# The first loads of an attention and mixture kernel spread over three queues, with eleven constant products ahead instead of fourteen

## The chip, the cores and the metric

The kernel runs on one core of one Trainium2 chip. The metric is device time in microseconds (us) from one execution; lower is less time. A core has TensorE (PE in the rows, its weight loads PEld), VectorE (DVE), ScalarE (ACT), GpSimd (POOL) and SyncE (SP). SP, ACT and POOL can each issue transfers (DMAs), each into a queue of its own.

## The reference

Three stages follow one another. Attention has batch 4, 12 heads, sequence 448 and head width 64, with capped scores; its output, as 1792 tokens of width 768, goes through a feed-forward layer with a squared ReLU, and that through a soft mixture of 8 experts with 4 slots each.

```python
scores = cap * np.tanh((q @ k.T / 8) / cap)
attn = softmax(scores);  x = attn @ v            # cap is one number, 30.0
g = s * np.maximum(x @ w_in, 0) ** 2 + b;  x = g @ w_out
logits = x @ phi                                  # 32 slots
d = softmax over tokens(logits);  slot_in = d.T @ x
slot_out[e] = np.maximum(slot_in[e] @ w1[e], 0) @ w2[e]
out = softmax over slots(logits) @ slot_out
```

## The kernel before

Two heads make a pair, so there are 24 pairs; for each pair q is a tile of 128 partitions by 448 (224 KB) and k one of 128 by 512 (256 KB). Each is split into a rounded part and a remainder (qh, ql, kh, kl), and a score tile is the sum of three products: kh with qh, kh with ql, kl with qh (`scores`, L148). ScalarE takes the tanh of a score tile (L158) and, when two pairs have delivered theirs, the exponential of both (L220). Sums, weighted values and the feed-forward products follow; the weights of the feed-forward layer are converted on the way (L391 to L430), and the tail reads the expert weights.

What the change touches lies ahead of all that, in `tile_kernel` (from L981). SP issues five loads in this order: `cap` into all 128 partitions (L993), then q and k of pair 0 into `c_tmp` and q and k of pair 1 into `c_hh` (L60, L61 of `load_qk`). DVE fills `c_ones` (L1000), and PE multiplies that constant with itself fourteen times into a PSUM tile that nothing reads (L1004); each product shows as two instructions in the trace. From `cap` DVE works out `c_acap`, the absolute value of cap (L1006, L1007), `c_flag` (whether it is at most 40, L1009), `c_tsc` and `c_eps` (L1011 to L1015, with one exponential on ACT, L1014). POOL issues five small loads: `c_cst`, two parts of `c_misc` (hot and phi), `c_s` and `c_b` (L1017 to L1024).

Every engine then loads `c_flag` into a register (L1035) and branches on it: one of two bodies runs, and nothing of a body runs ahead of that branch. In the body, `prep_pair` (L119 to L134) splits pairs 0 and 1 in parts: on DVE the order is qh and the first quarter of kh of pair 0, ql, the first quarter of kl, the rest of kh, then the first quarter of kh of pair 1 (L130), the rest of kl of pair 0, and ql and kl of pair 1; qh of pair 1 is cast on ACT (L128). SP's first transfers in the body are v (L119), q and k of pairs 2 and 3, v, and then the raw weights (L391). The tile framework plans the order on each engine ahead of time from priorities and its own estimate of when an input is there; queues and waits follow that plan.

Of the kernel before, what the change touches and what calls it, by code (L numbers as in the profile page):

```python
# [17 lines left out]
P = 128  # L18
# [39 lines left out]
def load_qk(nc, io, p, q2, k2):  # L58

    nc.sync.dma_start(q2, io["qT"][p])  # L60
    nc.sync.dma_start(k2, io["kT"][p])  # L61
# [920 lines left out]
@with_exitstack  # L982
def tile_kernel(ctx: ExitStack, tc: tile.TileContext, io):
    nc = tc.nc
    cp = ctx.enter_context(tc.tile_pool(name="cp", bufs=1, side="left"))
    c = {}

    def t(name, shape, dt=F32):
        c[name] = cp.tile(shape, dt, name="c_" + name)
        return c[name]  # L990

    cap = t("cap", [P, 1])
    nc.sync.dma_start(cap, io["cap"].partition_broadcast(P))  # L993
    tmp, hh = t("tmp", [P, 1312]), t("hh", [P, 2, 512])
    acc, pw = hh[:, 0, :], hh[:, 1, :]
    c["acc"], c["pw"] = acc, pw.rearrange("p (a b) -> p a b", b=NS)
    c["early"] = [(tmp[:, :S], tmp[:, S:S + KW]), (acc[:, :S], pw[:, :KW])]
    for g in range(2):
        load_qk(nc, io, g, *c["early"][g])
    nc.vector.memset(t("ones", [P, P]), 1.0)  # L1000
    with tc.tile_pool(name="warm", bufs=1, space=PSUM) as warm:
        w = warm.tile([P, P], F32, name="warm")
        for _ in range(14):
            nc.tensor.matmul(w, c["ones"], c["ones"], start=True, stop=True)  # L1004
    acap = t("acap", [P, 1])
    nc.vector.tensor_scalar(acap, cap, -1.0, None, op0=ALU.mult)  # L1006
    nc.vector.tensor_max(acap, acap, cap)  # L1007
    flag = t("flag", [1, 1], I32)
    nc.vector.tensor_scalar(flag, acap[0:1, :], CAP_FAST, None, op0=ALU.is_le)  # L1009
    tsc = t("tsc", [P, 1])  # L1010
    nc.vector.reciprocal(tsc, acap)  # L1011
    nc.vector.tensor_scalar(tsc, tsc, SCALE, None, op0=ALU.mult)
    eps = t("eps", [P, 1])
    nc.scalar.activation(eps, acap, AF.Exp, scale=-1.0)  # L1014
    nc.vector.tensor_scalar(eps, eps, EPS, None, op0=ALU.mult)  # L1015
    cst = t("cst", [P, 2, P])
    nc.gpsimd.dma_start(cst, io["cst"][:, 0:2, :])  # L1017
    c["idn"], c["fold"] = cst[:, 0, :], cst[:, 1, :]
    misc = t("misc", [P, KC * NS + 64])
    c["phi"], c["hot"] = misc[:, :KC * NS].rearrange("p (a b) -> p a b", b=NS), misc[:, KC * NS:].rearrange("p (a b) -> p a b", b=32)  # L1020
    nc.gpsimd.dma_start(c["hot"], io["hot"])
    for n in ("s", "b"):
        nc.gpsimd.dma_start(t(n, [P, 1]), io[n + "_"].partition_broadcast(P))
    nc.gpsimd.dma_start(c["phi"], io["phi"])  # L1024
    t("pbrow", [P, NS])
    t("z", [P, 1])
    t("pb", [P, 1])
    t("cl", [P, B, NCH, 32])
    f64 = io["w_in"].dtype == I64
    osc = None  # L1030
    dp = ctx.enter_context(tc.tile_pool(name="dp", bufs=1, space=DRAM))
    wsc = [dp.tile([P, KC * P], F32, name=f"wsc{i}") for i in range(FC)]
    if f64:
        osc = dp.tile([P, 3 * 4096], F32, name="osc")
    rv = nc.values_load(flag, min_val=0, max_val=1, skip_runtime_bounds_check_because="a comparison writes 0 or 1")  # L1035
    with tc.If(rv > 0) as br:
        Body(nc, tc, io, c, False, f64, wsc, osc).run()
    with br.Else():
        Body(nc, tc, io, c, True, f64, wsc, osc).run()
# [65 lines left out]
```

## Time and profile before

| | us |
|---|---|
| median of 3 runs | 618.41 |
| lowest and highest of them | 615.62, 619.05 |
| profiled execution | 618.13 |
| its span, from first to last instruction | 616.3 |

The profiled execution's time is 1.8 us longer than its span. The profile gives each engine's busy time, the instructions in order of time, what each waited for (in square brackets: idle time before it and what ended that), and for a transfer the time from issue to landing. Its rows on the first 16 us are the ones that matter here, since everything that the change edits runs there once.

### The profile page before, as it was taken

How to read it: one execution, taken by the hardware profiler on the slowest of the kernel's cores; microseconds unless marked ns; L12 is line 12 of the kernel's file. 1: busy time of each engine (PE TensorE's matmuls, PEld its weight loads, DVE VectorE, ACT ScalarE, POOL GpSimd, SP SyncE). 2: the span in 40 equal slices, each digit the busy share in tenths (PEclk: the TensorE clock that was granted, in tenths of full speed). 3: DMA queues.
4: the chain of work that ended last, by engine and by line, in shares of the span. 5: the costliest groups of instructions: out<-in, count | busy, mean ns of one | idle time of the engine just before them, and what ended most of it. 6: DMA issues, size and time to landing. Idle time of an engine off the chain costs nothing.

```text
span 616.3 us, 11164 instructions
## 1 busy us (share of the span) xinstructions
PE 573.2 (93%) x4488; PEld 386.5 (63%) x4488; DVE 382.7 (62%) x569; ACT 394.2 (64%) x611; POOL 4.1 (1%) x11
## 2 busy tenths in 40 slices
PE   7898999999999999989999999999999998999663
PEld 5243575657677576566875675858788874348543
DVE  4999999999894978748829867462422224213212
ACT  5899889889769688488697696946455541012001
POOL 1000000000000000000000000000000000000000
PEclk9999999999999999989999999999999999999977
DMA  8844768686684665556655632214979989999997
GB/s 293 282 136 144 265 237 294 223 296 220 203 293 155 223 214 160 171 199 194 202 186 173 208 118 75 69 53 151 349 256 307 342 316 365 417 420 414 420 412 279
DMA packets 49995, 149.97 MB, mean 243 GB/s; under 512 B 5504, under 2 KB 27792, under 8 KB 43024
## 3 DMA queue, kind: packets, MB, share of 16 engines
q1 hardware_dynamic: 49648, 148.66, 68.5%
q8 instruction: 37, 0.61, 0.4%
q0 software_dynamic: 288, 0.53, 0.2%
q14 instruction: 22, 0.18, 0.1%
HBM read 131.07 MB, written 18.09 MB: 242 GB/s over the span
## 4 chain that ended last, share of the span: by engine, by line
PE 47%; DMA 17%; DVE 16%; ACT 13%; issue 5%; SPq 1%; DVEq 0%; ACTq 0%
PE hp L557 24%; DMA wt<-in_w_dram 12%; PE U L261 6%; ACT e L220 4%; PE pt L682 2%; PE tp L587 2%; ACT e L182 2%; DVE ws L541 2%; ACT e L158 2%; PE sc L148 2%; DVE o L426 2%; PE sc L178 2%; DVE es L229 2%; PE L L601 1%; DVE rec L247 1%
## 5 line engine op out<-in xcount | busy, mean ns | idle before, releaser
L557 PE MATMUL hp<-x,ws 128*128 128x448 f32 x1152 | 269.2, 377 | 0.0
L557 PEld LDWEIGHTS hp<-x,ws 128*128 128x128 f32 x1152 | 208.1, 189 | 45.7 <-issue 30.6
L541 DVE TENSOR_TENSOR ws<-wr,ws 128x384 fp32r<-128x384 f32 x128 | 70.4, 553 | 88.1 <-ACT ws L540 81.1
L540 ACT CAST ws<-wr 128x384 fp32r<-128x384 f32 x128 | 65.6, 518 | 39.0 <-PE hp L557 38.3
L261 PE MATMUL U<-e,v 128*32 128x448 f32 (+1 forms) x672 | 69.0, 542 | 4.7 <-ACT e L220 3.6
L220 ACT ACTIVATE e<-e,c_acap 128x1792 f32<-128x1792 f32 (+1 forms) x42 | 71.2, 1696 | 0.5
L261 PEld LDWEIGHTS U<-e,v 128*32 128x32 f32 (+1 forms) x672 | 20.5, 109 | 42.9 <-issue 32.7
L590 ACT COPY g<-tp 128x384 f32<-128x384 f32 (+1 forms) x64 | 34.4, 538 | 13.2 <-PE tp L587 7.4
L565 ACT ACTIVATE r<-hp 128x448 f32<-128x448 f32 x63 | 34.4, 545 | 11.0 <-PE hp L557 9.9
L158 ACT ACTIVATE e<-sc,c_tsc 128x896 f32<-128x896 f32 x36 | 35.5, 1005 | 8.9 <-PE sc L148 8.9
L182 ACT ACTIVATE e<-sc,c_tsc 128x896 f32<-128x896 f32 x36 | 35.8, 1024 | 5.7 <-PE sc L178 5.5
L247 DVE RECIPROCAL rec<-rec 128x448 f32<-128x448 f32 x12 | 35.4, 2948 | 5.0 <-ACT rec L246 4.9
L566 ACT ACTIVATE r<-r 128x448 f32<-128x448 f32 x63 | 37.1, 588 | 0.5
L397 ACT ACTIVATE o<-raw 128x768 f32<-128x768 f32 x32 | 29.1, 931 | 12.2 <-DVE c_hh L693 7.4
L958 PE MATMUL so_ps<-wt,free 128*32 128x128 f32 x768 | 27.7, 295 | 9.2 <-DMA wt<-in_w_dram 9.2
L587 PE MATMUL tp<-c_cst,r 128*128 128x128 f32 x192 | 32.6, 277 | 3.6 <-ACT g L590 2.8
L942 ACT COPY wt<-op 128x512 f32<-128x512 f32 (+1 forms) x12 | 6.8, 568 | 42.6 <-PE op L937 42.5
L229 DVE TENSOR_TENSOR es<-e 128x1792 f32<-128x1792 f32 x12 | 24.3, 2022 | 14.1 <-ACT e L220 14.1
L587 PEld LDWEIGHTS tp<-c_cst,r 128*128 128x128 f32 x192 | 23.9, 141 | 12.7 <-ACT g L590 4.7
L430 DVE SCALAR_TENSOR_TENSOR o<-raw,o 128x768 int32<-128x768 int32 x32 | 30.4, 952 | 0.4
L426 DVE SCALAR_TENSOR_TENSOR o<-raw,o 128x768 int32<-128x768 int32 x32 | 30.4, 953 | 0.3
L958 PEld LDWEIGHTS so_ps<-wt,free 128*32 128x32 f32 x768 | 21.8, 117 | 13.3 <-DMA wt<-in_w_dram 9.5
(187 smaller groups left out, 695.0 us busy)
## 6 DMA issues: line engine op xcount, KB each, us to landing
wt<-in_w_dram SPq DMA_DIRECT2D x48, 1024.0 KB, 14.6
raw<-in_w_in_dram SPq DMA_DIRECT2D x16, 768.0 KB, 5.7
raw<-in_w_outT_dram SPq DMA_DIRECT2D x16, 768.0 KB, 5.8
raw<-in_w_out_dram SPq DMA_DIRECT2D x16, 768.0 KB, 5.7
wsc<-wr SPq DMA_DIRECT2D x16, 384.0 KB, 2.8
wr<-wsc SPq DMA_DIRECT2D x16, 384.0 KB, 3.4
osc<-o SPq DMA_DIRECT2D x16, 384.0 KB, 3.5
wr<-wsc SPq DMA_DIRECT2D x32, 192.0 KB, 3.2
```

Source lines behind the costliest of these rows:

```text
L158: nc.scalar.activation(self.e[Q][c][:, 2 * j:2 * j + 2, :], sc[:, :, :S], AF.Tanh, scale=self.c["tsc"])
L182: nc.scalar.activation(self.e[Q][c][:, 2 * j:2 * j + 2, :], sc[j][:, :, :S], AF.Tanh, scale=self.c["tsc"])
L220: ins = self.nc.scalar.activation(e, e, AF.Exp, scale=self.c["acap"]).ins
L247: nc.vector.reciprocal(self.rec, self.rec)
L261: products.append(lambda k=k, h=h, i=i, j=j, d=d: nc.tensor.matmul(self.U[j:j + 32, h, :S], self.v[2 * Q + i // 2][self.rows(i, k), d:d + ...
L426: nc.vector.scalar_tensor_tensor(o, raw[n][:, :, 1], -0x80000000, o, op0=ALU.bitwise_and, op1=ALU.bitwise_or)
L540: self.nc.scalar.copy(hi, u)
L541: self.nc.vector.tensor_sub(lo, u, hi.bitcast(F32))
L557: nc.tensor.matmul(hp[:, :S], ws[kc // 3][:, w, kc % 3, :], x[ORDER[kc] // 2][:, s, ORDER[kc] % 2, :], start=(k == 0), stop=(k == 3 * KC - 1))
L566: self.mark = nc.scalar.activation(r2, r2, AF.Square).ins
L587: nc.tensor.transpose(tp[:, q * P:(q + 1) * P], r2[:, 64 * odd + q * P:64 * odd + (q + 1) * P], self.c["idn"])
L958: nc.tensor.matmul(so_ps[32 * e:32 * e + 32, G, :], ht[G][:, f, 32 * e:32 * e + 32], w2[f // 4][:, f % 4, e, :], start=(f == 0), stop=(f = ...
```

## The change

Four edits, all ahead of the branch. `cap` is loaded by GpSimd's queue and stands first there, ahead of its five small loads. The two loads of q stay on SyncE's queue and are now the first in it. The two loads of k are issued by ScalarE, ahead of its first activation in the program's text. The constant products are eleven.

```diff
-    nc.sync.dma_start(cap, io["cap"].partition_broadcast(P))
+    nc.gpsimd.dma_start(cap, io["cap"].partition_broadcast(P))
...
     for g in range(2):
-        load_qk(nc, io, g, *c["early"][g])
+        nc.sync.dma_start(c["early"][g][0], io["qT"][g])
+        nc.scalar.dma_start(c["early"][g][1], io["kT"][g])
...
-        for _ in range(14):
+        for _ in range(11):
             nc.tensor.matmul(w, c["ones"], c["ones"], start=True, stop=True)
```

## Rows read from the trace of the kernel before

**Rows 1.** The page: shares of the chain that ended last, by engine.

```profile
PE 47%; DMA 17%; DVE 16%; ACT 13%; issue 5%; SPq 1%; DVEq 0%; ACTq 0%
```

**Rows 2.** That chain in order of time: start us, length us, what.

```profile
2.62 5.35 DMA c_hh<-in_kT_dram
...
9.28 0.70 PE sc L148 x4
10.00 1.02 ACT e L158
11.04 1.79 ACT e L220
```

**Rows 3.** Timeline of SP's queue: start us, us, engine, line, what.

```profile
0.74 0.40 SPq L993 DMA_DIRECT2D c_cap<-in_cap_dram  x1
...
2.62 0.43 SPq L61 DMA_DIRECT2D c_hh<-in_kT_dram  x1
4.92 0.80 SPq L119 DMA_DIRECT2D v<-in_v_dram  x2
...
8.15 0.90 SPq L391 DMA_DIRECT2D raw<-in_w_in_dram  x2
```

**Rows 4.** Transfers: issuer, count, KB each, us from issue to landing.

```profile
c_hh<-in_kT_dram SPq DMA_DIRECT2D x1, 256.0 KB, 5.4
...
c_cst<-in_cst_dram POOLq DMA_DIRECT2D x1, 128.0 KB, 3.8
...
c_cap<-in_cap_dram SPq DMA_DIRECT2D x1, 0.5 KB, 3.0
...
c_b<-in_b__dram POOLq DMA_DIRECT2D x1, 0.5 KB, 4.9
```

**Rows 5.** The same, whole trace: a late load on POOL with nothing ahead of it.

```profile
c_misc<-in_cst_dram POOLq DMA_DIRECT2D x1, 128.0 KB, 3.4
```

**Rows 6.** Stretches: length, busy time by engine (instructions), granted clock, DMA share, GB/s.

```profile
2.00:3.00 1.00, 1.00 (x7) 1.00 (x6) 0.00 (x0) 0.02 (x1) 1.00 (x3) 1.00 0.72 49
...
4.00:5.00 1.00, 1.00 (x6) 1.00 (x6) 0.53 (x5) 0.20 (x1) 0.02 (x1) 1.00 1.03 393
```

**Rows 7.** Timeline of DVE: start us, us, line, what, [idle before, releaser].

```profile
3.75 0.15 DVE L1006 TENSOR_SCALAR c_acap<-c_cap 128x1 f32<-128x1 f32 x1 [2.75 <-DMA c_cap<-in_cap_dram]
...
5.19 0.39 DVE L128 CAST qh<-c_tmp 128x448 fp32r<-128x448 f32 x1 [0.59 <-DMA c_tmp<-in_qT_dram]
5.82 0.23 DVE L130 CAST kh<-c_tmp 128x128 fp32r<-128x128 f32 x1 [0.24 <-DMA c_tmp<-in_kT_dram]
...
6.70 0.35 DVE L133 CAST kh<-c_tmp 128x384 fp32r<-128x384 f32 x1
7.99 0.23 DVE L130 CAST kh<-c_hh 128x128 fp32r<-128x128 f32 x1 [0.94 <-DMA c_hh<-in_kT_dram]
...
15.43 0.56 DVE L402 TENSOR_SCALAR wr<-wr 128x768 int32<-128x768 int32 x1 [3.12 <-ACT wr L397]
```

**Rows 8.** What touches the flag: count, ns min/median/max, first and last start us.

```profile
L1035 DVEq TENSOR_LOAD <-c_flag x1: 547/547/547, 4.4 to 4.4; - x1
```

**Rows 9.** Timeline of ACT: start us, us, line, what, [idle before, releaser].

```profile
0.74 1.28 ACT L1014 ACT_TABLE_LOAD   x1 [0.74 <-PEq L1095]
4.13 0.20 ACT L1014 ACTIVATE c_eps<-c_acap 128x1 f32<-128x1 f32 x1 [2.11 <-DVE c_acap L1007]
...
14.52 0.89 ACT L397 ACTIVATE wr<-raw 128x768 f32<-128x768 f32 x1
```

**Rows 10.** Timeline of POOL, the first two loads.

```profile
1.24 0.67 POOL L1017 DMA_DIRECT2D c_cst<-in_cst_dram  x1 [0.79 <-POOLq L1095]
1.91 0.53 POOL L1021 DMA_DIRECT2D c_misc<-in_hot_dram  x1
```

**Rows 11.** Readers of POOL's loads: the earliest is that of phi.

```profile
L479 PE MATMUL pp<-o,c_misc x96: 377/380/404, 62.9 to 214.1; 128*32 128x256 f32 x96
```

**Rows 12.** Timeline of PE.

```profile
1.06 5.98 PE L1004 MATMUL warm<-c_ones 128*128 128x128 f32 x28 [1.06 <-DVE c_ones L1000]
6.97 0.47 PE L148 MATMUL sc<-qh,kh 64*128 64x448 f32 x2
```

**Rows 13.** The constant products in 5.5:6 and 6.5:7: ns min/median/max, first and last start.

```profile
L1004 PE MATMUL warm<-c_ones x4: 421/422/422, 5.3 to 5.9; 128*128 128x128 f32 x4
...
L1004 PE MATMUL warm<-c_ones x5: 274/276/421, 6.1 to 6.8; 128*128 128x128 f32 x5
```

## The prediction

> **What bounds the kernel now.** I read the chain that ended last first, then the same chain in order of time over the first 30 us, then the timelines of each engine over that stretch. Over the whole run the chain is mostly PE with some DVE and ACT, and transfers own 17% of it [rows 1]. So an edit of the first microseconds counts only by how far it shifts the start of that chain. The start is plain: after SP's issues the chain is the transfer of k of pair 1, then its splitting on DVE, its score products, and from 10.00 the tanh and exponential on ACT [rows 2]. DVE has nothing to do for 0.94 us until that transfer lands, and goes on at 7.99 [rows 7]. From 10.00 through the first conversion at 14.52, ACT has no idle time [rows 2, 9]: whatever moves the tanh at 10.00 moves what follows.
>
> Why is that transfer late? It is issued fifth, at 2.62 [rows 3], and takes 5.4 us [rows 4], although the sixteen DMA engines move only 49 GB/s from 2 to 3 us, against 393 from 4 to 5 [rows 6]. From 2 to 3 they show a busy share of 0.72 with almost no bytes: that is cap, one 4-byte element for each of 128 partitions, which stands first in the same queue and lands 3.0 us after its issue [rows 3, 4]. The bulk waits behind it.
>
> A second gate lies nearby. Cap releases DVE at 3.75 [rows 7], the flag is worked out and read into a register (547 ns on DVE's sequencer, [rows 8]), and the first instruction of the body starts at 5.19 [rows 7]. The row names q of pair 0 as its releaser after 0.59 us of idle time, but the flag's read, started at 4.4, ends only at 4.95, and the branch comes after it; I take 5.19 − 3.75 = 1.44 us as the way from cap to the body. SP's first transfer of the body, at 4.92 [rows 3], has the same origin.
>
> **The loads of q and k.** They lose cap ahead of them and go out two by two. SP's q of pair 0 takes cap's place at 0.74; successive issues on SP stand (2.62 − 0.74)/4 = 0.47 us apart [rows 3], so q of pair 1 goes at 1.21. No row shows ACT issuing a transfer. If it does so at SP's pace, both k's are out by 1.7. If its table load of 1.28 us, which starts at 0.74 [rows 9], stays ahead of them, k of pair 1 goes out at 0.74 + 1.28 + 0.47 = 2.49; even that is a little earlier than 2.62. The volume is 2 × (224 + 256) KB = 0.98 MB, 2.5 us at 393 GB/s [rows 6]. Cap's 3.0 us with 0.5 KB [rows 4] bounds the fixed part from above, so issue at 1.21 plus 3.0 plus 2.5 makes 6.7 at the latest for everything, and with the table load ahead of k 2.49 + 3.0 + 0.7 (256 KB at that rate) = 6.2 for the last k if the rest is through by then. The lower end, with 2.0 us of fixed part, is 5.7. I take 6.0: it is then the body that is late, not the load.
>
> The Trainium skill speaks against this edit: "DMA: Bandwidth & Descriptors", section "Issuing engines are not separate DMA queues", says that transfers issued by different engines share the same sixteen DMA engines, so that spreading them saves issue time only. By that rule k of pair 1 would gain 2.62 − 1.21 = 1.4 us and land at 6.6 instead of 7.99; rows 6 speak for more, since the engines were not moving bytes while the bulk waited. The sum below is the same either way.
>
> **Cap on GpSimd's queue.** POOL's first issue is at 1.24 [rows 10], 0.50 us after SP's. No row shows a broadcast with nothing ahead of it on POOL. From below: SP's 3.0 us [rows 4] give a landing at 4.24. From above: 4.9 us, that of c_b, the same kind of broadcast, but with three loads ahead of it in its queue [rows 4], give 6.14. Between lie c_cst with 3.8, first in the queue but 256 times the bytes and beside the bulk, and the late load with 3.4 and nothing ahead [rows 4, 5]. I take 3.4, so cap lands at 4.64 and the body starts at 4.64 + 1.44 = 6.08 instead of 5.19: **0.89 us later**. Queued behind this wait are DVE's six small operations, c_eps on ACT, and the branch of every engine, hence all of the body, SP's loads included.
>
> The same page (section "Specifications") puts the first byte of GpSimd's path at about 1 us and that of SP's and ACT's at about 0.6. An estimate from these figures is 3.0 + 0.4 = 3.4 us, the value already taken from the late load.
>
> POOL's five other loads move back by one issue, 0.53 us [rows 10]. The earliest reader of any of them is at 62.9 [rows 11], so this is nothing; without that cover it would be 0.53.
>
> **ACT's two issues** take about 2 × 0.47 us and push the table load from 0.74 to about 1.7, its end from 2.02 to 3.0. ACT's next work, c_eps, waited for cap until 4.13 [rows 9] and now waits longer. Nothing; uncovered it would be 0.94.
>
> **Three products fewer.** The products run from 1.06 to 7.04, 5.98/14 = 0.427 us each, and the first score product starts at 6.97, right behind them [rows 12]. Eleven end at 1.06 + 11 × 0.427 = 5.76. That frees PE for pair 0, whose tanh is not on the chain (ACT idles before 10.00 for pair 1). Value: nothing, and nothing lost unless the clock suffers (a rival).
>
> **The sum.** With its loads landed, DVE runs from the body's start through pair 0's parts to k of pair 1 without waiting: 0.39 (L128), then 6.70 − 5.82 = 0.88 for L130 to L132, then 0.35 (L133), together 1.62 us [rows 7]. So L130 of pair 1 starts at 6.08 + 1.62 = 7.70 instead of 7.99, a shift of **−0.29 us**. What is late next is cap, no longer k. In general the shift is cap's landing minus 4.93; the lower landing, 4.24, gives −0.69, the upper, 6.14, gives +1.21. From 7.99 on the work is the same. SP's loads of the body start up to 0.89 us later, but in the trace of before they queue behind the last k, which leaves at 2.62 and lands at 7.99; now nothing is ahead. The raw weights, issued at 8.15 [rows 3], therefore land about as before, and ACT's conversion of them at 14.52 [rows 9] is not held up.
>
> Against the profiled execution (618.13, span 616.3 and 1.8 around it) this gives 618.13 − 0.29 = 617.84, say 617.8. That execution lies 0.28 under the median of the three runs, so against the median the same sum would be 618.1.
>
> **Rivals.**
> *A, the other side: cap becomes the bound.* If cap's landing takes 4.9 us after 1.24, the body starts at 7.58 and L130 of pair 1 at 9.20, 1.21 us later than now: 619.3. It decides at a landing of 4.93, 3.69 us after issue. For it: c_cst, at the same place in the same queue, needs 3.8, and the bulk of q and k now runs just then. Against it: cap has 0.5 KB, and c_b had three loads ahead.
> *B, the clock.* Granted clock reads 1.00 from the start [rows 6], but the products' own rows take 422 ns until about 6 us and 274 at the end [rows 13]: the rise from 1.2 to 2.4 GHz came late in the products, after more than 5 us of unbroken work. Eleven end at 5.76, before that. If the rise is missed, the products of pair 1 on the chain (0.70 us, [rows 2]) take up to 1.4: +0.7 on −0.29, giving 618.5. The first score products follow the eleven after about half a microsecond and speak against a long delay.
> *C, the plan.* The framework orders each engine's work from its own estimate of arrivals, and these change. The trace cannot show another order; the largest wait of DVE in this stretch, 3.12 us [rows 7], is my bound both ways: 614.7 to 621.0 on the forecast, beside which the run-to-run spread of 615.62 to 619.05 lies.
> *D, no effect on k:* ACT's loads come out late behind the table load. Worked out above: the time stays 617.8, since cap then decides anyway. It is part of the forecast.
>
> **How the numbers follow.** Forecast with D: 0.55. A: 0.17. B: 0.10. C: 0.18, a little more on the faster side, since the median lies near the top of its three runs. A change of 0.5% is 3.1 us, about what a measurement of this kernel can tell from no change. The forecast, A and B all lie within it; of C about half goes beyond on the faster side (0.10) and a third on the slower (0.06). So faster 0.10, same 0.84, slower 0.06. The range takes in cap's two bounds (617.4 to 619.3), the spread of the runs and part of C: 615.2 to 619.8.
>
> **What would show each step.** Cap: DVE's first operation on it near 4.64. The body: L128 1.44 us after that. K: no wait before L130 of pair 1, and the SP and ACT queues moving near 390 GB/s well before 4 us. ACT: two issues ahead of the table load. PE: an idle stretch between 5.76 and the first score, and the products' durations telling when the clock rises. The chain: tanh of pair 1 near 9.7 in place of 10.00. I am wrong if cap lands well away from 4.64, or if the order of the body's work beyond 30 us differs and with it the time by more than about 1 us.

## The result and the profile after

| | before | changed | ratio, 95% interval |
|---|---|---|---|
| median of 20 runs each, us | 616.75 | 621.67 | 1.0068 [1.0052, 1.0084] |
| once more on another chip (27 and 6 runs), us | 617.63 | 623.41 | 1.0089 [1.0061, 1.0118] |
| profiled execution, us | 618.13 | 623.47 | |
| its span, us | 616.3 | 621.7 | |

The change costs 0.7% to 0.9%, 4 to 6 us. (The ratios here and below are not those of the two medians, which stand 4.9 and 5.8 us apart in this table.) On each engine the instructions stand in the same order as before, apart from the moved loads and the three missing products, so the loss is in when things happen and not in what is done.

The page's chain that ended last, by engine (for [rows 1]), has less PE and more transfers:

```profile
PE 42%; DMA 20%; DVE 16%; ACT 14%; issue 5%; SPq 1%; DVEq 0%; ACTq 0%
```

Transfers of the changed kernel (issuer, count, KB each, us from issue to landing), for [rows 4]:

```profile
c_tmp<-in_kT_dram ACTq DMA_DIRECT2D x1, 256.0 KB, 3.7
c_hh<-in_kT_dram ACTq DMA_DIRECT2D x1, 256.0 KB, 4.3
...
c_hh<-in_qT_dram SPq DMA_DIRECT2D x1, 224.0 KB, 4.6
...
c_cap<-in_cap_dram POOLq DMA_DIRECT2D x1, 0.5 KB, 4.7
```

The bulk gained a little more than forecast: k of pair 1 is issued at 1.17 and needs 4.3 us instead of 5.4, so it lands at 5.5, where 6.0 was forecast and the kernel before has 7.97 [rows 2]. Cap needs 4.7 us instead of 3.0. The timelines of POOL's, SP's and ACT's queues show when each was issued, for [rows 3, 9, 10]:

```profile
1.25 0.67 POOL L993 DMA_DIRECT2D c_cap<-in_cap_dram  x1 [0.81 <-POOLq L1096]
```

```profile
1.21 0.44 SPq L999 DMA_DIRECT2D c_hh<-in_qT_dram  x1
7.18 0.80 SPq L119 DMA_DIRECT2D v<-in_v_dram  x2
...
10.40 0.90 SPq L391 DMA_DIRECT2D raw<-in_w_in_dram  x2
```

```profile
1.17 0.45 ACTq L1000 DMA_DIRECT2D c_hh<-in_kT_dram  x1
1.65 1.28 ACT L1015 ACT_TABLE_LOAD   x1 [1.65 <-PEq L1096]
6.38 0.20 ACT L1015 ACTIVATE c_eps<-c_acap 128x1 f32<-128x1 f32 x1 [3.44 <-DVE c_acap L1008]
...
11.31 1.01 ACT L158 ACTIVATE e<-sc,c_tsc 128x896 f32<-128x896 f32 x1 [0.60 <-PE sc L148]
12.36 1.79 ACT L220 ACTIVATE e<-e,c_acap 128x1792 f32<-128x1792 f32 x1
14.05 1.89 ACT L158 ACTIVATE e<-sc,c_tsc 128x896 f32<-128x896 f32 x2
17.27 0.89 ACT L397 ACTIVATE wr<-raw 128x768 f32<-128x768 f32 x1 [1.33 <-DMA raw<-in_w_in_dram]
```

And DVE, for [rows 7]; the third row is the first part of k of pair 1, the step on which the sum was made:

```profile
6.00 0.15 DVE L1007 TENSOR_SCALAR c_acap<-c_cap 128x1 f32<-128x1 f32 x1 [4.99 <-DMA c_cap<-in_cap_dram]
...
7.43 0.39 DVE L128 CAST qh<-c_tmp 128x448 fp32r<-128x448 f32 x1 [0.59 <-issue]
...
8.88 0.22 DVE L130 CAST kh<-c_hh 128x128 fp32r<-128x128 f32 x1
...
33.45 2.95 DVE L247 RECIPROCAL rec<-rec 128x448 f32<-128x448 f32 x1 [0.63 <-ACT rec L246]
```

The last of these in the trace of before:

```profile
30.30 2.95 DVE L247 RECIPROCAL rec<-rec 128x448 f32<-128x448 f32 x1 [0.62 <-ACT rec L246]
```

Everything of q and k has landed by 5.8 (q of pair 1, 1.21 + 4.6), before cap's value is used at 6.00. The body waits for cap alone: it starts at 7.43 instead of 5.19. From there the delay can be followed along the run against the trace of before: k's first part +0.89 (8.88), the tanh of pair 1 +1.31 (11.31), the exponential +1.32 (12.36), the first conversion of raw weights +2.75 (17.27, after a wait of 1.33 for the transfer that was not there before), the first reciprocal +3.15 (33.45; before it starts at 30.30). After that it moves by steps, up more than down, to the 5.4 of the span.

Why the raw weights come late is seen in a table of stretches (columns as in [rows 6]). First the changed kernel, then the one before:

```profile
7.00:8.00 1.00, 0.00 (x0) 0.00 (x0) 0.57 (x3) 0.56 (x1) 0.00 (x0) 0.71 0.02 5
8.00:10.00 2.00, 1.89 (x8) 1.14 (x8) 2.00 (x6) 0.29 (x1) 0.00 (x0) 0.50 0.81 244
10.00:12.00 2.00, 1.88 (x12) 1.46 (x10) 1.14 (x4) 1.40 (x2) 0.00 (x0) 0.50 0.90 251
12.00:14.00 2.00, 1.86 (x10) 0.83 (x6) 1.89 (x4) 1.97 (x2) 0.00 (x0) 0.50 1.10 324
```

```profile
7.00:8.00 1.00, 0.85 (x7) 0.46 (x6) 0.06 (x2) 0.22 (x2) 0.00 (x0) 1.00 1.02 376
8.00:10.00 2.00, 1.19 (x9) 0.89 (x10) 1.97 (x6) 0.90 (x1) 0.00 (x0) 1.00 1.05 383
10.00:12.00 2.00, 1.45 (x12) 0.68 (x8) 1.93 (x5) 1.97 (x2) 0.00 (x0) 1.00 1.10 407
12.00:14.00 2.00, 1.11 (x12) 0.42 (x16) 0.32 (x1) 2.00 (x3) 0.00 (x0) 1.00 1.02 418
```

Before, the body's loads follow the last k closely (247 GB/s from 6 to 7 us), and the transfers run at 376 GB/s and more from 7 us on. After, the queues are empty between q and k and the body's first load: 5 GB/s from 7 to 8, and 244 to 324 for the next six us. Raw weights, issued 2.25 us later, take 6.8 us instead of 6.2 to land, at 17.25. Before, they landed at 8.15 + 6.2 = 14.35, and ACT took them at 14.52: they had 0.17 us to spare. The first raw tile's transfer, before and after:

```profile
raw<-in_w_in_dram SPq DMA_DIRECT2D x1, 768.0 KB, 6.2
```

```profile
raw<-in_w_in_dram SPq DMA_DIRECT2D x1, 768.0 KB, 6.8
```

The clock column shows the second thing: 0.50 from 8 to 14, which is 1.2 GHz, while the kernel before holds 2.4 GHz there. The products end at 5.18 and PE is idle for about three us. Its rows, for [rows 12], show score products of 0.57 to 0.74 us where they took 0.36 to 0.47:

```profile
1.06 4.12 PE L1005 MATMUL warm<-c_ones 128*128 128x128 f32 x22 [1.06 <-DVE c_ones L1001]
8.11 0.74 PE L148 MATMUL sc<-qh,kh 64*128 64x448 f32 x2 [2.93 <-DVE kh L130]
8.62 0.67 PE L148 MATMUL sc<-ql,kh 64*128 64x448 f32 x2
9.09 0.57 PE L148 MATMUL sc<-qh,kl 64*128 64x448 f32 x2
```

The rise itself was not missed. The eleven products go from 421 ns to 275 ns (minimum, median and maximum of those from 3.6 us on are below), at about 4.0 us and so sooner than in the kernel before (about 6.5, [rows 13]). They end at 5.18 instead of the 5.76 forecast; what follows them is the idle stretch, and then products at the lower clock.

```profile
L1005 PE MATMUL warm<-c_ones x11: 275/275/421, 3.6 to 4.9; 128*128 128x128 f32 x11
```

### The profile page after: what moved, and what is told of

It reads as the page before. It is cut to its first block, busy times and chain, and to the rows that moved or that the text cites. A ratio compares the mean times of both kernels' runs of the same rounds, so it can differ in the third digit from the quotient of the medians.

```text
span 621.7 us, 11151 instructions
## 1 busy us (share of the span) xinstructions
PE 578.6 (93%) x4482; PEld 387.6 (62%) x4482; DVE 383.0 (62%) x569; ACT 394.9 (64%) x611; POOL 4.6 (1%) x12
## 4 chain that ended last, share of the span: by engine, by line
PE 42%; DMA 20%; DVE 16%; ACT 14%; issue 5%; SPq 1%; DVEq 0%; ACTq 0%
PE hp L557 20%; DMA wt<-in_w_dram 12%; PE U L261 6%; ACT e L220 4%; DVE ws L541 2%; DMA raw<-in_w_outT_dram 2%; DMA raw<-in_w_in_dram 2%; DVE o L426 2%; PE pt L682 2%; PE tp L587 2%; ACT e L182 2%; DMA osc<-o 2%; ACT e L158 2%; PE sc L178 2%; PE sc L148 2%
## 5 line engine op out<-in xcount | busy, mean ns | idle before, releaser
L397 ACT ACTIVATE o<-raw 128x768 f32<-128x768 f32 x32 | 29.0, 928 | 12.3 <-DMA osc<-o 9.4
```

## The experiments

Two theories were set against each other. The late body: cap lands late because the bulk of q and k now runs beside it, the body starts late, and SP's loads with it. The clock: eleven products leave PE idle ahead of the scores, and the granted clock falls. Where an expectation says theory 1 or T1, the first is meant, theory 2 or T2 the second; other rivals are described where they stand. Edits are against the kernel before unless said otherwise. Every ratio is to the kernel before on the same chip, with its 95% interval; where the later course of the run is told, it is that of one profiled execution.

**Cap alone, on POOL's queue.**

```diff
-    nc.sync.dma_start(cap, io["cap"].partition_broadcast(P))
+    nc.gpsimd.dma_start(cap, io["cap"].partition_broadcast(P))
```

> The kernel before with one edit: cap is loaded by GpSimd's queue; q and k stay on SyncE's, fourteen products. Theory T1 (the body waits for cap, and GpSimd's queue brings cap late): cap lands at 5 to 6 us instead of 3.7, the body's first DVE instruction starts at 6.4 to 7.5, the first conversion on ACT 1.5 to 2.8 us later than 14.5, and the time is 2 to 4 us over before (about 619 to 621 against 616.8). Rival T2 (the loss comes from the fewer products and the clock): the time is within 1 us of before. Rival T3 (two hardware queues hold GpSimd's transfers up): with one hardware queue cap lands by about 4.6 and the loss is under 1 us.

Measured 621.45 against 618.21, 1.0063 [1.0041, 1.0086]. Cap's first use is at 5.86, the conversion at 16.75 after a wait of 1.38 for its transfer. This one line, with fourteen products and q and k on SP, gives nearly the loss of the whole change. And it needs no low clock: the granted clock of its trace is 1.00 in every stretch from 8 to 18 us, the score products take 0.36 to 0.47 us, and the first reciprocal is 3.6 us late all the same (33.88).

```profile
8.00:10.00 2.00, 1.56 (x8) 0.74 (x8) 2.00 (x7) 0.87 (x1) 0.00 (x0) 1.00 0.90 271
10.00:12.00 2.00, 1.48 (x12) 1.06 (x14) 1.00 (x3) 1.36 (x3) 0.00 (x0) 1.00 0.96 246
```

**K alone, on ACT's queue**, cap first on SP as before.

```diff
-        load_qk(nc, io, g, *c["early"][g])
+        nc.sync.dma_start(c["early"][g][0], io["qT"][g])
+        nc.scalar.dma_start(c["early"][g][1], io["kT"][g])
```

> The kernel before with one edit: the first loads of k are issued by ACT; cap stays first on SyncE's queue, fourteen products. T1: cap lands at about 3.7 to 4.0, the body starts at about 5.2 to 5.5, k of pair 1 has landed by then, so its first cast starts near 6.8 instead of 8.0 and the time is 0.7 to 1.2 us under before. Rival (the sixteen DMA engines are shared, so a second queue only saves issue time and may slow cap): within 0.5 us of before, or slower if cap lands later than 4.4.

Measured 620.64 against 618.21, 1.0034 [1.0007, 1.0061]. DVE's timeline:

```profile
5.33 0.15 DVE L1007 TENSOR_SCALAR c_acap<-c_cap 128x1 f32<-128x1 f32 x1 [4.33 <-DMA c_cap<-in_cap_dram]
```

Cap was issued at 0.74 on SP, as before, ahead of everything in its queue, and was used at 5.33 instead of 3.75. The gain that theory 1 expected here didn't come; the rival's delay did. So it isn't POOL's queue that makes cap slow, but bulk that another queue issues no later than cap (here k at 0.74 on ACT).

**The changed kernel without the four loads of q and k** (the first two pairs then work on zeros, so this part of the attention is left out).

```diff
-    for g in range(2):
-        nc.sync.dma_start(c["early"][g][0], io["qT"][g])
-        nc.scalar.dma_start(c["early"][g][1], io["kT"][g])
+    nc.vector.memset(tmp[:, :S + KW], 0.0)
+    nc.vector.memset(hh, 0.0)
```

> The changed kernel without the four first loads of q and k: VectorE fills their tiles with zeros, so that pairs 0 and 1 are computed on zeros. Cap is on GpSimd's queue and eleven products run, as in the changed kernel. This measures cap's way from GpSimd's issue to its landing with nothing else moving. Theory T1a (cap's 128 small elements wait behind the bulk of q and k): cap lands within 3.4 us of its issue at 1.25, so by 4.7, and the body starts near 6.1 or earlier. Rival T1b (GpSimd's path takes this long by itself): 4.5 us or more, cap at 5.8 to 6.0 as in the changed kernel.

```profile
4.17 0.15 DVE L1006 TENSOR_SCALAR c_acap<-c_cap 128x1 f32<-128x1 f32 x1 [1.09 <-DMA c_cap<-in_cap_dram]
...
5.53 0.39 DVE L128 CAST qh<-c_tmp 128x448 fp32r<-128x448 f32 x1 [0.52 <-issue]
```

From the same issue at 1.25 on POOL cap is there 2.9 us later, 1.8 us sooner than with the bulk beside it. That is shown, then: the bulk delays cap. The time of this one run, 621.46, doesn't follow: the body starts only 0.34 us later than before, yet the conversion waits 1.19 for its transfer and starts at 15.78. Here too SP's queue was empty ahead of the body's loads. The zero fills also hold the constant products back (they end at 8.20), though pair 1's tanh, at 9.96, is not late.

**Eleven products alone**, twice.

```diff
-        for _ in range(14):
+        for _ in range(11):
```

> The kernel before with one edit: eleven constant products instead of fourteen. T2 (the products and the clock are the loss): TensorE idles from about 5.8 to the first scores, the clock is at its lower level in a part of the first 25 us, and the time is 1.5 to 4 us over before. T1: the scores follow the products after about 0.3 us as the body starts at 5.2, so the time is within 0.7 us of before.

> The kernel before with eleven products, as in e3_eleven_only (0.27%, interval from 0 to 0.55%), once more. Theory 2, that fewer products cost by the clock: mean clock near 0.980 again and 0.2 to 0.4% slower. Rival, that the first result was spread alone: within 0.1%.

Measured 1.0027 [1.0000, 1.0055] and then 0.9994 [0.9969, 1.0019]: between them no loss is shown, and 0.3% is about the most that it could be.

**The changed kernel with fourteen, and with twenty-two products.**

```diff
-        for _ in range(11):
+        for _ in range(14):
```

> The changed kernel with fourteen products again (cap on GpSimd's queue, k on ACT's). T1: cap still lands at about 6.0 and the body starts at about 7.4; the products end near 7.0 or earlier, so TensorE idles less than 1.5 us and the clock may stay up; the time is 0.3 to 1.5 us under the changed kernel's (about 620 to 621.4), still 3 to 4.5 us over before. T2: the loss is gone and the time is within 1 us of before.

> The changed kernel with twenty-two constant products, so that TensorE stays busy until the body starts at 7.4; cap and k as in the changed kernel. If the clock between 7.7 and 14.5 us cost time (T2), the exponentials and conversions up to 30 us come earlier than in the changed kernel and the time is 1 to 2 us under its 621.7 (relative to before: +0.3 to +0.5%). If the front is bound by cap and the raw weights (T1), the first conversion stays near 17 us and the time within 0.7 us of the changed kernel's (+0.55 to +0.8% over before).

Measured 1.0054 [1.0029, 1.0078] with fourteen and 1.0046 [1.0028, 1.0064] with twenty-two. With twenty-two the clock was up from 6.9 to 20.5 us, and the conversion still started at 17.61, after a wait of 2.11 for its transfer. With fourteen it is up from 8 to 18 us. The conversion stays late as theory 1 expected, while the 0.46% lies in the band that theory 2 gave. Keeping the clock up leaves 0.46 to 0.54% of the 0.68 to 0.89%; the intervals overlap, so it isn't shown that it gives back anything.

**The late body alone.** Nothing is moved; twelve multiplications by one hold cap back on DVE.

```diff
+    for _ in range(12):
+        nc.vector.tensor_scalar(cap, cap, 1.0, None, op0=ALU.mult)
```

> The kernel before with twelve chained multiplications by one of the 128 x 1 tile cap put ahead of its first use: the body starts about 2.3 us later (DVE's first instruction of the body at about 7.5 instead of 5.19), all queues and the fourteen products as before, and q and k all landed by then. Theory 1 (the late start of the body is what costs): SP's body loads are issued about 2.3 us later, ACT's first conversion of raw weights starts 2 to 3 us later than 14.52 and then waits for its transfer, the first reciprocal comes 2 to 3 us later than 30.6, the time rises by 2 to 4 us (0.3 to 0.6%). Rival (what costs in the changed kernel is the clock after fewer products, and the late body is absorbed as it only meets loads that were late anyway): under 1.2 us.

Measured 621.06 against 617.63, 1.0057 [1.0034, 1.0081]. DVE, SP's queue and ACT:

```profile
6.12 0.15 DVE L1008 TENSOR_SCALAR c_acap<-c_cap 128x1 f32<-128x1 f32 x1
...
7.55 0.39 DVE L128 CAST qh<-c_tmp 128x448 fp32r<-128x448 f32 x1 [0.59 <-issue]
```

```profile
10.51 1.19 SPq L391 DMA_DIRECT2D raw<-in_w_in_dram  x2
```

```profile
16.91 0.90 ACT L397 ACTIVATE wr<-raw 128x768 f32<-128x768 f32 x1 [1.03 <-DMA raw<-in_w_in_dram]
```

The body starts 2.36 us late, the conversion 2.39 us, the first reciprocal 2.74 us (33.04), the time is up 3.4 us. SP's queue stood empty here too, and the stretches after it look like those of the changed kernel:

```profile
8.00:10.00 2.00, 1.59 (x8) 0.80 (x8) 2.00 (x7) 0.61 (x1) 0.00 (x0) 1.00 0.77 233
10.00:12.00 2.00, 1.72 (x10) 1.35 (x10) 1.26 (x4) 1.14 (x2) 0.00 (x0) 0.63 0.86 235
12.00:14.00 2.00, 1.80 (x8) 0.84 (x6) 1.41 (x4) 1.97 (x3) 0.00 (x0) 0.51 1.07 383
```

With every load on its old queue and in its old place, lateness of the body is enough to make most of the loss (0.57% of 0.68 to 0.89%). The clock column falls here too, to 0.63 and 0.51, in spite of the fourteen products, so this run alone doesn't set the clock aside. That is done by the kernels that have a late body at a granted clock of 1.00 from 8 to 18 us: cap alone, k alone, and the change with fourteen and with twenty-two products. They lose 0.34 to 0.63%.

**The late body and eleven products, no load moved** (both edits above).

> The kernel before with the twelve chained multiplications of e12_late_body ahead of cap's first use and eleven products: both suspected causes, and none of the moved loads. If the late body and fewer products are all there is, it repeats the changed kernel: first conversion of raw weights near 17.3, clock at 0.50 over most of 8 to 14 us, mean clock near 0.977, time up by 0.7 to 0.9% (4.3 to 5.5 us). If the moved loads cost something of their own, by their queues, it stays at the 0.57% of the late body alone.

Measured 620.61 against 617.62, 1.0049 [1.0023, 1.0074]; conversion at 17.24, clock 0.50 from 10 to 16. Its front repeats that of the changed kernel, but the time is no worse than with fourteen products: the sum of two causes that I expected isn't there. By the expectation this would leave a cost of the moved loads themselves, but the intervals overlap that of the changed kernel, so no such cost is shown.

**Four and twenty-two products**, nothing else (the diff as above with 4 and 22).

> The kernel before with four products on the constant in place of fourteen, nothing else. Theory 2 (fewer products cost by the granted clock): the first 25 us show long stretches at 0.50, the mean clock falls below the 0.983 of the kernel before to about 0.977, as in the two kernels with eleven products and the changed front, and the time rises by 2 to 4 us (0.3 to 0.6%). Rival (the late body alone costs): within 1 us of the kernel before, 617 to 619.

> The kernel before with twenty-two products on the constant: the products end at about 9 us instead of 7.04 and hold the first score product for up to 2 us, the score products then run at the higher clock. Theory 1: pair 1's tanh moves from 10.00 by less than 1 us, and with it the first conversion; time within 1.5 us of before. Theory 2 (more products keep the clock up later on): mean clock at or above 0.984 and the time not above the kernel before by more than 0.5 us in spite of the later scores.

Measured 1.0044 [1.0026, 1.0063] and 1.0026 [1.0003, 1.0048]. With four, the score products took the long durations up to 12.3 us, yet the exponential moved from 11.04 only to 11.33 and the first reciprocal by 0.3; where the other 2.2 us of the median arose isn't settled. In time this is what theory 2 expected, in the mean clock (0.983) not: that fewer products cost something by another way stays open for four; for eleven it is little or nothing, as measured above. With twenty-two the products end at 7.57, the clock is up, pair 1's tanh comes at 9.73, and nothing is gained.

**The changed kernel again**, on the chip of the late body.

> The changed kernel itself, once more beside the other three on one chip: 0.5 to 0.8% slower than the kernel before. If theory 1 and theory 2 each hold a part, the losses of the late body (e12_late_body) and of fewer products (eleven alone: 0.27%) add up to it within 0.2%.

Measured 1.0089 [1.0061, 1.0118]; cap at 6.25, body at 7.69, conversion at 17.58 after a wait of 1.38, first reciprocal 4.4 us late.

**Other ways to bring cap, k or the raw weights earlier.** Cap as one element, first on SP, spread over the partitions by a product on PE, with twelve constant products around it instead of fourteen:

```diff
-    nc.sync.dma_start(cap, io["cap"].partition_broadcast(P))
+    nc.sync.dma_start(cap1, io["cap"].partition_broadcast(1))
...
+            last = nc.tensor.matmul(wc, c["ones"][0:1, :], cap1, start=True, stop=True)
...
+        nc.vector.tensor_copy(cap, wc)
```

> The kernel before, but cap comes as a single element, first in SyncE's queue, and TensorE spreads it to 128 partitions by a product with the constant after the fifth of twelve constant products; q and k follow on SyncE's queue as before. If the 128 small elements cost cap its 3.0 us and hold the bulk up (T1), cap lands at 2.5 to 3.0, the body starts at 4.2 to 4.8, q and k land 0.5 to 1 us earlier, the first conversion comes 0.7 to 1.5 us before 14.5 and the time is 0.5 to 1.5 us under before. If the fixed part of a transfer is all that counts, cap lands near 3.7 and the time is within 0.5 us of before.

Measured 1.0023 [1.0001, 1.0045]. DVE and ACT:

```profile
5.73 0.40 DVE L128 CAST qh<-c_tmp 128x448 fp32r<-128x448 f32 x1 [0.59 <-issue]
```

```profile
15.32 0.89 ACT L397 ACTIVATE wr<-raw 128x768 f32<-128x768 f32 x1 [1.51 <-DMA raw<-in_w_in_dram]
```

The gain that was expected didn't come: cap is used at 4.30, later than before, and the body starts 0.54 us late. K of pair 1 no longer waits: its first part is at 7.18 and the tanh at 9.18, 0.8 us sooner than before. This is the case that the prediction described, a body somewhat late and k early. But the raw weights, issued 0.54 us later (8.69), land 0.95 us later (15.30), and the conversion waits 1.51 for them. So the very gain that the prediction was about, had it come, would have been lost at the raw weights.

Q and k of pair 1 on ACT, placed behind its table load and one activation in the program, cap first on SP:

```diff
-    for g in range(2):
-        load_qk(nc, io, g, *c["early"][g])
+    load_qk(nc, io, 0, *c["early"][0])
...
+    first = nc.scalar.activation(t("first", [P, 1]), c["ones"][:, 0:1], AF.Exp)
+    with tc.issue_after(first.ins):
+        for a, b in zip(c["early"][1], (io["qT"][1], io["kT"][1])):
+            nc.scalar.dma_start(a, b)
```

> The kernel before, but q and k of pair 1 are issued by ACT behind its table load and one small activation, so after 2.0 us, when cap's elements are already moving; cap, then q and k of pair 0 stay on SyncE's queue, fourteen products. T1 (cap has to go out before any bulk): cap lands by 4.0, the body starts at 5.2 to 5.5, k of pair 1 lands near 6.5 instead of 8.0, its first cast starts near 6.9, the first conversion 0 to 0.8 us before 14.5, and the time is 0 to 1 us under before. Rival (any bulk on a second queue delays cap): cap lands at 4.4 or later, and the time is 1 us or more over before.

Measured 1.0002 [0.9978, 1.0026]. The trace shows the two loads issued at 1.05 and 1.48, while the table load runs, and not after 2.0 as expected; that is still 0.3 us behind cap's issue on SP at 0.74. Cap is used at 3.80: bulk that another queue issues this much later doesn't delay it. The conversion has no wait (15.23), but k of pair 1 is not early either (first part at 8.38 instead of 7.99), so nothing is gained.

The first raw tile ahead of v on SP, in the kernel before, in the changed one, and with cap spread by PE:

```diff
-        for n in range(self.raws - 1):
+        load(0)
+        yield
+        for n in range(1, self.raws - 1):
...
+                    next(self.conv)
```

> The kernel before with one edit: the body's first transfer on SyncE is the first raw weight tile (ahead of v), so that it lands earlier; some steps around it move in the planned order. Everything ahead of the branch is as before. This is the control for the next two. ACT did not wait for that tile in the kernel before (no idle time ahead of 14.5 us), so the time is within 0.4% of before; a gain of over 1 us would say that the tile bound the front already.

> The changed kernel with the same edit: first raw tile ahead of v. Theory T1 (the late body costs twice: 1.3 us at the first exponential, and 1.4 us more because the raw tile lands late): ACT no longer waits 1.3 us for the raw tile, the first conversion comes at 15.5 to 16.3 instead of 17.3, and the time lies 1 to 2 us over the control, about half of the 4 us that the change costs without the edit. Rival (the raw tile's lateness is absorbed later, and the loss is elsewhere): the same distance to the control as without the edit, 3 to 4.5 us.

> Cap as a single element first on SyncE's queue and spread by TensorE, as in p1, and the first raw tile ahead of v. In p1 the scores of pair 1 came 0.8 us early and ACT then waited 1.5 us for the raw tile. T1: without that wait the first conversion comes at 13.5 to 14.2 (14.5 before), and the time is 0.5 to 1.5 us under before and under the control. Rival: no gain, within 0.5 us of the control.

Measured 1.0004 [0.9980, 1.0027], 1.0075 [1.0047, 1.0102] and 1.0005 [0.9976, 1.0033]. ACT then converts at 11.41 in the changed kernel and at 10.34 in the kernel before, so the gap between them shrinks from 2.75 to 1.07 us. The changed front still starts its body at 7.36, and its first reciprocal is 1.4 us behind that of the same edit on the kernel before. The loss of 4 us is there all the same (the changed kernel has six runs here), where half of it was expected, and I can't say where the rest of it arises. So the raw weights are where the delay grows in the changed kernel, but ordering them first doesn't cure the late body. None of these versions beats the kernel before.

## Why the prediction was wrong

The forecast was 617.8 with a range to 619.8, and 0.06 on slower by over 0.5%. It came to 621.67, slower by 0.68%. The kernel before itself came to 616.75 in twenty runs, 1.7 us under the three runs that the forecast had; the shift was forecast at -0.29 us and is 4.9.

- **Cap's landing: the term that was mis-sized.** Taken at 3.4 us after issue, from the late load [rows 5], it was 4.7. The bounds, 3.0 and 4.9, held it; the choice between them was wrong. The late load ran while the engines moved 157 GB/s (214.8 to 218.2 us); cap runs where four transfers of q and k start (392 GB/s from 4 to 5). The row for that was at hand: c_cst, first in the same queue and beside the bulk, 3.8 [rows 4]. The text held its 256-fold bytes against it, when the company counted. Without the company cap takes 2.9 on POOL, no longer than the 3.0 on SP before, so the 0.4 us that the estimate added for POOL's path doesn't show in the landing. With bulk on another queue that was issued ahead of it or with it, cap takes 4.5 to 5.0 in seven traces, on POOL and on SP alike. The rule that the prediction cited for k (the Trainium skill, "DMA: Bandwidth & Descriptors", "Issuing engines are not separate DMA queues") also says that transfers of different issuers interleave on the same engines. This trace agrees: the small load lost beside the bulk. I weighed the rule for k and not for cap.
- **The point of decision was nearly right.** It was put at a landing of 4.93; the landing of about 6.0 is past it, and the body followed 1.43 us behind (1.44 forecast). The parts ahead of k's first one took 1.45 us instead of the 1.62 added up, as their rows overlap (7.43 + 0.39 is past 7.74). Rival A (a landing at 6.14, body at 7.58, k's first part at 9.20) names the mechanism. What came was 6.00, 7.43 and 8.88. The prediction's own formula with cap at 6.00 gives a shift of +1.07 and 619.2, which is inside its range: cap alone doesn't explain the miss.
- **"The raw weights therefore land about as before": the step that failed.** It is the reason why A was priced at 1.21 and not at 3. The reasoning saw that v is no longer behind k, and took it that a load issued later would then take less time. SP's issues of the body start 2.26 us later, one by one, 0.47 us apart, and the queue has nothing to send meanwhile. To land as before, the raw weights would have had to take 2.25 us less; they took 0.6 more, at 244 to 324 GB/s instead of 383 to 418. I hadn't read their landing before: 14.35, only 0.17 us ahead of ACT. With that margin, any delay of their landing beyond 0.17 us reaches ACT unless ACT is late as well. In the changed kernel this adds 1.43 us (+1.32 at the exponential, +2.75 at the conversion). The step fails at a smaller lateness too: with cap spread by PE the body is 0.54 us late and the raw weights 0.95. In the time, what is shown is the late body as a whole (0.57% by itself); the share of the raw weights in it isn't, as the changed kernel with raw weights first still loses 0.75%.
- **The clock (rival B)** came on top of A, but not as B had it. The rise that it feared to miss came at about 4.0 us, while the products ran; the lower clock stands behind 2.93 us of idle PE. B put that gap at about half a microsecond; by the sum's own terms it was 6.70 - 5.76 = 0.94. The score products then took 0.57 us and longer, and from k's first part to the tanh it is 2.43 us instead of 2.01: 0.42, where up to 0.7 had been allowed.
- **From 7.99 on "the work is the same"**: the same in order, but not in time. In the traces of the eight kernels whose body starts 1.6 to 2.5 us late (cap alone moved, k alone moved, the change with eleven, fourteen and twenty-two products and with raw weights first, the late body with fourteen and with eleven) the first reciprocal starts at 32.7 to 34.7; with eleven (twice), four and twenty-two products and the body on time it starts at 30.1 to 31.9. So most of the loss seems to be made in the first 33 us, though these are single executions and don't order the times: with q and k of pair 1 on ACT behind cap it starts at 32.3, and nothing is lost. To its +3.15 there the profiled run adds another 2.2 by its end, and this isn't the front's: two of the larger steps stand where its clock falls, near 270 us (granted 0.50 to 0.73 from 270 to 278; before 0.50 to 0.66 from 266 to 270) and near 518 (0.50 to 0.64 from 516 to 520; before 1.00), and there are others of about one us, up near 100 and down near 360 and 600; other kernels' runs have such steps too, up and down. Six of the eight kernels lose 0.34 to 0.63%. The changed kernel loses 0.68 and 0.89%, and 0.75% with raw weights first. The difference, one or two us, is open; the intervals overlap. Less clock may be in it: the six sets of runs with eleven products have a mean clock of 0.976 to 0.980, those with fourteen 0.981 to 0.985. But the late body with eleven, and the second set of runs with eleven alone, show no loss by it, and the set with four has 0.983.
- **Right:** k early and without a wait; ACT's two issues ahead of the table load, hidden (its next work waits for cap until 6.38); POOL's other loads, hidden; the order on every engine, so no part for rival C.

## What to carry to other kernels

A tiny load that gates everything belongs on the wire before any bulk, and its time is read from a transfer that runs in the same company, not from one that runs alone. Before a start is allowed to slip, read the landing of each transfer behind it against its reader: an engine without a wait may have 0.17 us to spare, and an early arrival elsewhere doesn't pay for it. A late start can cost more than its own shift: here the raw weights were issued 2.25 us later and landed 2.9 us later.

## What the runs showed of the hardware that was not expected

- A load of one 4-byte element for each of 128 partitions takes 2.9 us alone on POOL and 3.0 on SP with bulk behind it in its own queue. With bulk that another queue issued ahead of it or with it, it takes 4.5 to 5.0 on POOL (six traces) and 4.6 on SP; with bulk that another queue issued 0.3 us behind it, 3.0 on SP.
- From 8 to 12 us, right after SP's queue had run empty, the transfers moved 233 to 251 GB/s, in the changed kernel and with the late body alone, at a busy share of 0.77 to 0.90; the same loads behind a running queue moved 383 to 407 at 1.05 to 1.10. It isn't a slow climb: in the changed kernel the rate is 351 GB/s from 9 to 9.5 us and falls to 203 from 10 to 10.5. Nor is an empty queue needed: with cap spread by PE the transfers never stopped (162 GB/s from 6 to 7), and from 8 to 12 they moved 274 and 327. Why the rate is low isn't settled.
- The granted-clock column can read 1.00 while PE runs at the low clock. With four products, PE's timeline and the stretch say:

```profile
1.06 2.08 PE L1004 MATMUL warm<-c_ones 128*128 128x128 f32 x8 [1.06 <-DVE c_ones L1000]
6.17 0.74 PE L148 MATMUL sc<-qh,kh 64*128 64x448 f32 x2 [3.03 <-DVE kh L130]
...
10.05 0.57 PE L148 MATMUL sc<-qh,kh 64*128 64x448 f32 x2
```

```profile
10.00:12.00 2.00, 2.00 (x12) 1.27 (x12) 1.93 (x5) 1.68 (x2) 0.00 (x0) 1.00 1.09 403
```

Its score products take the same 0.57 as those of the changed kernel at a granted 0.50. Before the first rise the durations tell the clock, and the column doesn't.
